# Clustered attention and two feed-forward layers: three weight pieces decoded in place, one multiply on another engine, and a new order around tiles 6 to 9

## Chip, cores and metric

One core of a Trainium2 chip runs the whole program. The metric is device microseconds of one execution, given as the median of several runs. Engines are named as in the profile: PE does matmuls (PEld is its loading of weights), DVE is the vector engine, ACT the scalar engine, POOL is GpSimd, and SP issues most of the DMAs, one after the other.

## What is computed

The reference has three stages, all in float32:

- Attention over 2 batches, 8 heads, 768 positions and 64 channels. Each query and key is assigned to the nearest of 16 centroids of its head (by cosine), and a query sees only keys of its own cluster. Scores are q k^T / 8, masked, then a softmax, then the product with v.
- A feed-forward layer on the 1536 x 512 result: h = x w_in (512 to 2048), a rational function P(h)/Q(h) of degree 3 over 2, then the product with w_out (2048 to 512).
- A mixture of eight experts (512 to 1024, relu, 1024 to 512). Their weights are a softmax over the experts, normalised eight times over rows and columns.

## The kernel before

Matmuls run in a reduced float32 form, so an operand is kept as a high part and a low part and one product takes three matmuls (lines 860 to 862). A weight tile is therefore "decoded" or "split" into two tiles, wh and wl.

**Attention** walks 8 pairs of heads (pair n is one batch and two heads). The loop counter is kk, 12 steps to a pair, 96 in all; in what follows "step x" is kk modulo 12. In each step kk PE makes scores of one tile of 128 queries against 768 keys (lines 391 and 392), DVE takes their maxima (397), ACT the exponential (405); four steps later PE transposes them (421), ACT and DVE split the transposed tile into high and low (430, 431), and three steps after that PE multiplies with v (444, 445). Operands of the next pairs are prepared by a list of pieces, one per step: transposes and splits of q and k (240, 250, 251), similarity to the centroids (264), and the choice of cluster in four steps: classify_m (284), classify_c (288, 289), classify_d (293) and classify_e (297), at steps 5 to 8. In classify_c the product `sv` is made on POOL, except for the first pair. The one-hot result goes through ACT (315, tile OHM) and four small DMAs (319) into the score operands sq2 and sk2 of the next pair; they are issued in step 10 and read by the first scores of the next pair.

SP is one queue in the order of the program. Per pair it issues: four loads of q and k for the pair after next (131, step 0); tb, which moves half of a result across partitions (514, steps 0, 3, 6 and 9); ten moves of operands st1, sq2, sk2 (336 to 340, in two groups, steps 2 and 3); rinv and rb, the reciprocals of the row sums (487, 491, step 3); v (138, step 4); the four OHM moves (319, step 10). POOL does, per pair, four additions x1f = ta + tb that wait for the tb move (515, issued two steps after it), twice the three operations of x_out (522 to 524, steps 8 and 9), and the split of v (350, 351; steps 4 and 10).

**Weights of the feed-forward layer** come as 32-bit words in pairs (`[..., 0]` and `[..., 1]`). decode has six operations: high and low on ACT (684, 687), shift on DVE (690), whole, upper and rest on POOL (693, 696, 699). Four half pieces, both halves of (0, 0) and of (0, 1) (unit, first or second weight), are decoded inside the attention loop by piece_w (729 to 752), with tiles of their own: raw, emag and etop, one buffer each. Their loads are issued at kk = 14, 28, 42 and 56; the six operations follow at 7 to 12 steps after. All other weights go through load_w, split_w and dp (661, 703): weight (1, 0) is loaded at kk = 88, weight (1, 1) at kk = 94; (1, 0) is decoded in five steps at kk = 100, in the list `end` (778) and at t = 1, 2, 3 of the next stage, and (1, 1) at t = 2 to 6.

**Feed-forward** has 48 tiles (512 tokens by 128 hidden units; tile n belongs to a unit of 256 hidden units). A step t issues, in the order of the program: act_b of tile t - 1 (901 to 906: square, abs, two affine forms on ACT, two products on POOL), act_steps of tile t - 2 and act_q of tile t - 1 on DVE, pieces of weights (key "w"), act_r of tile t - 1 (914, 915, ACT), then on PE stage1 of tile t (12 matmuls, tile h) and stage2 of tile t - 5 (12 matmuls into two tiles y). The results y of one step are emptied in the next one (list `late`). PSUM has three banks for y (h of tiles 0 to 2 use them first), three for h and two for q. A bank of h comes free with the last of act_steps (926).

At the seam, attention's PSUM pools (ps_s two tiles of two banks, ps_t two banks, ps_v and ps_p one each) are handed on to the three pools of the next stage. `rb_last` is a ps_s tile for the last reciprocals, `pt_31` another for transposes of the last group; rb_last is read by x_last (474).

Of the kernel before, what the change touches and what calls it, by code (L numbers as in the profile page):

```python
# [30 lines left out]
def kernel(  # L31
# [15 lines left out]
    nc = tc.nc  # L47
# [42 lines left out]
    def left(name, bufs):  # L90
        return ctx.enter_context(tc.tile_pool(name=name, bufs=bufs, reuse_waits="tile"))
# [84 lines left out]
        nc.vector.tensor_tensor(WG[:, :, E : 2 * E], wg, WG[:, :, 0:E].bitcast(F32), op=ALU.subtract)  # L176


    csq = one.tile([P, D], F32, name="csq")
    css = one.tile([P, 16], F32, name="css")[:, :1]  # L180
    nc.scalar.activation(csq, cen, AF.Square, accum_out=css)
    cnm = one.tile([P, 16], F32, name="cnm")[:, :1]
    gt(cnm, css, half[:, 0:1], op=ALU.pow)
    nc.vector.tensor_scalar(cnm, cnm, 1e-6, None, op0=ALU.add)
    crn = one.tile([P, 32], F32, name="crn")[:, :1]
    nc.vector.reciprocal(crn, cnm)
    cn2 = one.tile([P, 2, D], F32, name="cn2")
# [26 lines left out]
    def prep(n):  # L214
# [71 lines left out]
        def classify_c():  # L286
            sv = st["sv"] = one.tile([P, NB, C], F32, tag="sv", name=f"sv_{n}")
            nc.vector.tensor_tensor(sv, st["sims"], bc(st["mx"]), op=ALU.is_equal)
            (nc.vector.tensor_tensor if n == 0 else gt)(sv, sv, rev, op=ALU.mult)

        def classify_d():
            mk = st["mk"] = one.tile([P, 32], F32, tag="mk", name=f"mk_{n}")[:, :NB]
# [116 lines left out]

    def transposes(g, part):  # L410
        pss = []
        if g == NG - 1 and part == 0:
            last["pt"] = ps_s.tile([P, 2, 512], F32, tag="s", name=f"pt_{g}")
        for j in (2 * part, 2 * part + 1):
            if g == NG - 1 and part != 1:
                ps = last["pt"][:, j % 2]
            else:
                ps = ps_t.tile([P, 512], F32, tag="t", name=f"pt_{g}_{j}")
            for i in range(GT):
                pv_ = prob[g][i].rearrange("p a b -> p (a b)")  # L420
# [105 lines left out]
    def attention():  # L526
# [38 lines left out]
        for kk in range(END + LAGT + 9):  # L565
# [86 lines left out]
    def source(ui, i):  # L652
        m, e, u = units[ui]
        fs = slice(u * FU, (u + 1) * FU)
        if m == 0:
            src = moe_w_in[:, fs] if i == 0 else moe_w_out[fs, :]
            return src.bitcast(U32).rearrange("(c p) (f w) -> p c f w", p=P, w=2)
        src = moe2_w1[e][:, fs] if i == 0 else moe2_w2[e][fs, :]
        return src.rearrange("(c p) f -> p c f", p=P)

    def load_w(ui, i):
        if ui >= len(units):
            return
        if units[ui][0] == 0:
            t = stg.tile([P, *wshape[i], 2], U32, tag=f"stg{i}", name=f"stg_{ui}_{i}")
        else:
            t = sg2.tile([P, *wshape[i]], F32, tag=f"sg{i}", name=f"sg_{ui}_{i}")
        nc.sync.dma_start(t, source(ui, i))
        staged[ui, i] = t

    def weight_tiles(ui, i):
        shape = [P, *wshape[i]]
        return (
            wp[ui % 2].tile(shape, F32R, tag=f"wh{i}", name=f"wh_{ui}_{i}"),
            wp[ui % 2].tile(shape, F32R, tag=f"wl{i}", name=f"wl_{ui}_{i}"),
        )

    def decode(raw, mag, top, wh, wl):
# [47 lines left out]
    LASTK = 2 * NT * (NPR - 1)  # L726
    early = {}

    def piece_w(x, i, h):
        st = {}  # L730
        n = wshape[i][0] // 2
        c = slice(h * n, (h + 1) * n)
        shape = [P, n, wshape[i][1]]

        def load():
            st["raw"] = etp.tile([*shape, 2], U32, tag="raw", name=f"raw_{i}_{h}")
            nc.sync.dma_start(st["raw"], source(0, i)[:, c])

        def begin():
            if h == 0:  # L740
                weights[0, i] = weight_tiles(0, i)
            mag = etp.tile(shape, F32, tag="emag", name=f"emag_{i}_{h}")
            top = etp.tile(shape, F32, tag="etop", name=f"etop_{i}_{h}")
            st["fns"] = decode(st["raw"], mag, top, *(w[:, c] for w in weights[0, i]))

        early.setdefault(x, []).append(load)
        early.setdefault(x + 7, []).append(begin)
        for y, k in enumerate((7, 8, 9, 10, 11, 12)):
            early.setdefault(x + k, []).append(lambda y=y: st["fns"][y]())

    for y in range(4):
        piece_w(14 + 14 * y, y // 2, y % 2)

    mctx = ctx.enter_context(ExitStack())
    wp = [left("wp_0", 1)]
    etx = ctx.enter_context(ExitStack())
    etp = etx.enter_context(tc.tile_pool(name="etp", bufs=1, reuse_waits="tile"))
    for kk in attention():
        if isinstance(kk, list):
            end = kk  # L760
            break
        if kk == LASTK:
            pctx.close()
            etx.close()
            wp.append(left("wp_1", 1))
            stg = mctx.enter_context(tc.tile_pool(name="stg", bufs=1, reuse_waits="tile"))
            dp = mctx.enter_context(tc.tile_pool(name="dp", bufs=2, reuse_waits="tile"))
        if kk == LASTK + 4:
            load_w(1, 0)
        if kk == LASTK + 10:  # L770
            load_w(1, 1)
        for fn in early.pop(kk, ()):
            fn()
        if kk == GT * NG + 4:
            ahead = [(split_w(1, 0), 0), (split_w(1, 1), 1)]
            ahead[0][0].pop(0)()
    assert not early
    end.insert(1, ahead[0][0].pop(0))
    for fn in end:
        fn()  # L780
    sctx.close()
# [117 lines left out]
    def act_b(n):  # L899
        ps, q0, h2, uu, ww, _, _ = act[n]  # L900
        nc.scalar.activation(h2, ps, AF.Square)
        nc.scalar.activation(q0, ps, AF.Abs, scale=cf[:, 4:5])
        nc.scalar.activation(uu, ps, AF.Identity, scale=cf[:, 3:4], bias=cf[:, 2:3])
        nc.scalar.activation(ww, ps, AF.Identity, scale=cf[:, 1:2], bias=cf[:, 0:1])
        gt(uu, uu, h2, op=ALU.mult)  # L905
        gt(uu, uu, ww, op=ALU.add)
# [329 lines left out]
    for ui in range(NO):  # L1236
# [39 lines left out]
    for t in range(last):  # L1276
        if t == N1 + 2:
# [24 lines left out]
        for a in p.get("s1", ()):  # L1302
            stage1(*a)
        for fn in p.get("g", ()):
            fn()
        for ui, c, f in p.get("s2", ()):
            for i in range(4 * f // FT, 4 * (f + 1) // FT):
                stage2(ui, c, i)
# [45 lines left out]
```

## Time and profile before

| | |
|---|---|
| median of 3 runs | 1561.09 us (1558.44 to 1562.6) |
| the profiled execution | 1559.76 us |
| its span, first to last instruction | 1557.9 us |
| PE busy | 1529.0 us, 98% of the span |
| DVE, ACT, POOL busy | 1129.6, 650.2, 742.4 us |
| attention, from the span's start to the first matmul of tile 0 | 271.1 us |
| feed-forward, tiles 0 to 47 | to about 560 us |
| mixture of experts | the rest |

The profiled execution is 1.3 us under the median of the runs. The span leaves 1.9 us of the execution's time outside. PE's busy time counts matmuls from start to a modelled end, and those ends overlap with the next start, so a delay is read from the spacing of starts and from the idle time in brackets behind a row, not from the busy share. A bracket names what ended the idle time.

### The profile page before, as it was taken

What the parts mean: (1) busy time and instruction counts of PE and PEld (TensorE: products, weight loads), DVE (VectorE), ACT (ScalarE), POOL (GpSimd) and SP (SyncE); (2) the same over time, 40 slices, a digit from 0 to 9 for tenths busy, and PEclk for the clock granted to TensorE, in tenths of its full rate; (3) what the DMA queues carried; (4) which work ended last, traced back from release to release, by engine and by line L of the source; (5) the groups of instructions that cost most, each with busy time, mean ns of one, the idle gap of its engine ahead of it and who ended that gap; (6) DMA issues with size and microseconds to landing.
All of it is one profiled execution on the core that took longest, in us unless ns stands there. A gap on an engine that the chain in (4) does not pass through costs nothing.

```text
span 1557.9 us, 20894 instructions
## 1 busy us (share of the span) xinstructions
PE 1529.0 (98%) x7807; PEld 1351.4 (87%) x7807; DVE 1129.6 (73%) x1909; ACT 650.2 (42%) x1238; POOL 742.4 (48%) x633
## 2 busy tenths in 40 slices
PE   7999998899999999999999999999999999999998
PEld 5889898688888787888989999999999999998997
DVE  7888888678888748786666666667666666676666
ACT  5888887888887521221212121212121212121211
POOL 2254452888788763443444344434443444344420
PEclk9999999899999999999999999999999999999999
DMA  8567742211220010110011001101110101010102
GB/s 186 139 160 163 173 100 73 82 54 55 82 82 1 28 41 15 41 41 27 28 41 42 27 29 40 41 28 34 34 41 28 41 28 41 28 41 28 41 1 82
DMA packets 72574, 89.04 MB, mean 57 GB/s; under 512 B 30116, under 2 KB 50424, under 8 KB 72472
## 3 DMA queue, kind: packets, MB, share of 16 engines
q1 hardware_dynamic: 70904, 87.31, 20.3%
q8 instruction: 61, 1.00, 0.3%
q10 hardware_dynamic: 1568, 0.39, 0.1%
q14 instruction: 41, 0.34, 0.1%
HBM read 62.57 MB, written 3.19 MB: 42 GB/s over the span
## 4 chain that ended last, share of the span: by engine, by line
PE 91%; DVE 4%; POOL 2%; ACT 2%; issue 1%; DMA 1%; SPq 0%; ACTq 0%; POOLq 0%; DVEq 0%
PE y L860 14%; PE y L861 14%; PE y L862 14%; PE m L862 9%; PE m L860 9%; PE m L861 9%; PE pt L421 4%; PE h L861 4%; PE h L860 4%; PE h L862 4%; PE v L444 2%; PE v L445 2%; PE s L391 2%; PE s L392 2%; PE sim L264 1%
## 5 line engine op out<-in xcount | busy, mean ns | idle before, releaser
L972 DVE SCALAR_TENSOR_TENSOR acc<-y,gate,acc 128x512 f32<-128x512 f32 x348 | 260.8, 750 | 177.4 <-PE y L862 176.0
L860 PE MATMUL y<-wh,gh 128*128 128x512 f32 x696 | 270.9, 389 | 1.6 <-DVE acc L972 1.6
L862 PE MATMUL y<-wh,gl 128*128 128x512 f32 x696 | 271.9, 391 | 0.0
L861 PE MATMUL y<-wl,gh 128*128 128x512 f32 x696 | 271.8, 390 | 0.0
L1089 POOL TENSOR_TENSOR rl<-sg,rh 128x512 fp32r<-128x512 f32 x29 | 45.7, 1576 | 399.9 <-ACT rh L1081 399.9
L1166 ACT COPY c<-m 128x384 f32<-128x384 f32 x58 | 27.9, 482 | 455.9 <-PE m L862 455.9
L860 PEld LDWEIGHTS y<-wh,gh 128*128 128x128 f32 x696 | 130.7, 188 | 28.3 <-DVE acc L972 2.5
L862 PEld LDWEIGHTS y<-wh,gl 128*128 128x128 f32 x696 | 130.6, 188 | 27.3
L861 PEld LDWEIGHTS y<-wl,gh 128*128 128x128 f32 x696 | 130.6, 188 | 26.1
L1151 DVE SCALAR_TENSOR_TENSOR gl<-v,gh 128x384 fp32r<-128x384 f32 x174 | 119.4, 686 | 0.0
L1150 ACT ACTIVATE gh<-v 128x384 fp32r<-128x384 f32 x174 | 91.5, 526 | 60.9 <-DVE v L1189 29.2
L431 DVE TENSOR_TENSOR ptl<-pt,pth 128x384 fp32r<-128x384 f32 x192 | 97.6, 550 | 23.7 <-ACT pth L430 23.0
L860 PE MATMUL h<-XH,wh 128*128 128x512 f32 x264 | 104.3, 395 | 7.9 <-POOL uu L905 5.7
L714 POOL TENSOR_SCALAR wh<-sg 128x512 fp32r<-128x512 f32 x70 | 44.2, 631 | 136.9 <-PE y L862 131.4
L1150 ACT ACTIVATE gh<-u 128x384 fp32r<-128x384 f32 x58 | 30.6, 527 | 184.0 <-DVE u L1175 184.0
L861 PE MATMUL h<-XL,wh 128*128 128x512 f32 x264 | 104.3, 395 | 0.2 <-POOL XL L1300 0.2
L862 PE MATMUL h<-XH,wl 128*128 128x512 f32 x264 | 104.2, 395 | 0.0
L715 POOL TENSOR_TENSOR wl<-sg,wh 128x512 fp32r<-128x512 f32 x70 | 99.1, 1415 | 5.8
L430 ACT CAST pth<-pt 128x384 fp32r<-128x384 f32 x192 | 83.5, 489 | 38.2 <-PE pt L421 36.2
L397 DVE TENSOR_REDUCE nm<-s 128x1 f32<-128x768 f32 x96 | 91.3, 951 | 8.4 <-PE s L392 8.2
L405 ACT ACTIVATE pr<-s,nm 128x768 f32<-128x768 f32 x96 | 88.5, 922 | 3.2 <-DVE nm L397 3.1
L421 PE MATMUL pt<-ident,pr 128*128 128x128 f32 x576 | 83.2, 277 | 4.5 <-DVE ptl L431 4.4
(231 smaller groups left out, 4093.5 us busy)
## 6 DMA issues: line engine op xcount, KB each, us to landing
sg<-in_moe_w_dram SPq DMA_DIRECT2D x64, 512.0 KB, 3.4
stg<-in_moe_w_in_dram SPq DMA_DIRECT2D x7, 1024.0 KB, 5.4
stg<-in_moe_w_out_dram SPq DMA_DIRECT2D x7, 1024.0 KB, 5.4
st<-HQK SPq DMA_DIRECT2D x15, 384.0 KB, 4.5
qk<-in_q_dram SPq DMA_DIRECT2D x16, 192.0 KB, 3.6
vt<-in_v_dram SPq DMA_DIRECT2D x8, 384.0 KB, 5.0
out_dram<-acc SPq DMA_DIRECT2D x12, 256.0 KB, 2.0
st<-LQK SPq DMA_DIRECT2D x15, 192.0 KB, 4.6
```

The lines of the kernel that those rows point to most:

```text
L397: nc.vector.tensor_reduce(nm, ps[:, :, :HS], axis=AX.XY, op=ALU.max, negate=True)
L405: nc.scalar.activation(pr, ps[:, :, :HS], AF.Exp, bias=nm, accum_out=rss[n][:, x : x + 1])
L421: nc.tensor.transpose(ps[:, i * P : (i + 1) * P], pv_[:, j * P : (j + 1) * P], ident)
L430: nc.scalar.copy(th[:, jj, :], ps[:, :HS])
L431: nc.vector.tensor_tensor(tl[:, jj, :], ps[:, :HS], th[:, jj, :].bitcast(F32), op=ALU.subtract)
L715: gt(wl[:, c], raw[:, c], wh[:, c].bitcast(F32), op=ALU.subtract)
L860: nc.tensor.matmul(ps, ah, bh, start=first, stop=False)
L861: nc.tensor.matmul(ps, ah, bl, start=False, stop=False)
L862: nc.tensor.matmul(ps, al, bh, start=False, stop=last)
L972: nc.vector.scalar_tensor_tensor(a, ps, p, a, op0=ALU.mult, op1=ALU.add)
L1150: nc.scalar.activation(gh[:, f], c, AF.Relu)
L1151: soon.append(lambda: nc.vector.scalar_tensor_tensor(gl[:, f], c, 0.0, gh[:, f].bitcast(F32), op0=ALU.max, op1=ALU.subtract))
```

## The change

Six parts:

1. The three small tiles css, cnm and crn become columns of one tile, and the square of the centroids is written into cn2, which is overwritten later. This saves space.
2. sv is multiplied on DVE for every pair.
3. For group 30 the last two transposes go into a ps_s tile as well, and rb_last is taken two steps later, at kk = 98. As tiles alternate between the two buffers of ps_s, rb_last then lies in banks 0 and 1 (before: 2 and 3) and pt_31 in banks 2 and 3. The first h tile lies in bank 3 in both.
4. piece_w decodes in place: mag is raw[..., 1] and top is raw[..., 0], so emag and etop are gone, and the space goes to a pool for the first weight of odd units (wp_1a). It takes six half pieces, of (0, 0), (0, 1) and now (1, 0). Loads are issued at kk = 11, 23, 35, 47, 59 and 71, the six operations at 6, 7, 7, 8, 11 and 11 steps after, which is at steps 5, 6, 6, 7, 10 and 10 of the next pair. The tile raw has one buffer, as before. Weight (1, 0) is no longer decoded at the seam; (1, 1) is loaded at kk = 88 and decoded at t = 3 to 7.
5. act_b makes uu before q0.
6. In steps t = 5, 6 and 7 stage1 and stage2 are issued ahead of the activations and y is emptied at once; in t = 6, 7 and 8 stage2 comes before stage1. PE's order is then, with hN for stage1 of tile N and yN for stage2: h5 y0 y1 h6 y2 h7 y3 h8 h9 y4 (before: h5 y0 h6 y1 h7 y2 h8 y3 h9 y4).

```diff
@@ -176,15 +176,13 @@
-    css = one.tile([P, 16], F32, name="css")[:, :1]
...
+    crs = one.tile([P, 32], F32, name="crs")
+    css, cnm, crn = crs[:, 0:1], crs[:, 8:9], crs[:, 16:17]
+    cn2 = one.tile([P, 2, D], F32, name="cn2")
+    nc.scalar.activation(cn2[:, 0, :], cen, AF.Square, accum_out=css)
...
@@ -286,7 +284,7 @@
-            (nc.vector.tensor_tensor if n == 0 else gt)(sv, sv, rev, op=ALU.mult)
+            nc.vector.tensor_tensor(sv, sv, rev, op=ALU.mult)
@@ -409,10 +407,10 @@
-        if g == NG - 1 and part == 0:
+        if (g, part) in ((NG - 2, GT - 1), (NG - 1, 0)):
             last["pt"] = ps_s.tile([P, 2, 512], F32, tag="s", name=f"pt_{g}")
         for j in (2 * part, 2 * part + 1):
-            if g == NG - 1 and part != 1:
+            if g == NG - 2 and part == GT - 1 or g == NG - 1 and part != 1:
                 ps = last["pt"][:, j % 2]
@@ -584,7 +582,7 @@
-            elif kk == END:
+            elif kk == END + 2:
                 last["rb"] = ps_s.tile([P, 2, 512], F32, tag="s", name="rb_last")
@@ -670,9 +668,10 @@
+        pool = wp[ui % 2 * (1 + i)]
         return (
-            wp[ui % 2].tile(shape, F32R, tag=f"wh{i}", name=f"wh_{ui}_{i}"),
...
+            pool.tile(shape, F32R, tag=f"wh{i}", name=f"wh_{ui}_{i}"),
...
@@ -726,33 +725,34 @@
-            st["raw"] = etp.tile([*shape, 2], U32, tag="raw", name=f"raw_{i}_{h}")
-            nc.sync.dma_start(st["raw"], source(0, i)[:, c])
+            st["raw"] = etp.tile([P, n, wshape[i][1], 2], U32, tag="raw", name=f"raw_{ui}_{i}_{h}")
+            nc.sync.dma_start(st["raw"], source(ui, i)[:, c])
...
-            mag = etp.tile(shape, F32, tag="emag", name=f"emag_{i}_{h}")
-            top = etp.tile(shape, F32, tag="etop", name=f"etop_{i}_{h}")
-            st["fns"] = decode(st["raw"], mag, top, *(w[:, c] for w in weights[0, i]))
-
-        early.setdefault(x, []).append(load)
-        early.setdefault(x + 7, []).append(begin)
-        for y, k in enumerate((7, 8, 9, 10, 11, 12)):
+            raw = st["raw"]
+            st["fns"] = decode(
+                raw, raw[..., 1].bitcast(F32), raw[..., 0].bitcast(F32), *(w[:, c] for w in weights[ui, i])
+            )
+
+        early.setdefault(x - 1, []).append(load)
+        early.setdefault(x + 5, []).append(begin)
+        for y, k in enumerate((5, 6, 6, 7, 10, 10)):
             early.setdefault(x + k, []).append(lambda y=y: st["fns"][y]())
 
-    for y in range(4):
-        piece_w(14 + 14 * y, y // 2, y % 2)
+    for y, (ui, i) in enumerate(((0, 0), (0, 1), (1, 0))):
+        for h in range(2):
+            piece_w(2 * NT * (2 * y + h + 1), ui, i, h)
...
-    wp = [left("wp_0", 1)]
+    wp = [left("wp_0", 1), left("wp_1a", 1)]
@@ -762,20 +762,15 @@
-            wp.append(left("wp_1", 1))
+            wp.append(left("wp_1b", 1))
...
         if kk == LASTK + 4:
-            load_w(1, 0)
-        if kk == LASTK + 10:
             load_w(1, 1)
...
-        if kk == GT * NG + 4:
-            ahead = [(split_w(1, 0), 0), (split_w(1, 1), 1)]
-            ahead[0][0].pop(0)()
     assert not early
-    end.insert(1, ahead[0][0].pop(0))
+    ahead = split_w(1, 1)
@@ -899,8 +894,8 @@
         nc.scalar.activation(h2, ps, AF.Square)
+        nc.scalar.activation(uu, ps, AF.Identity, scale=cf[:, 3:4], bias=cf[:, 2:3])
         nc.scalar.activation(q0, ps, AF.Abs, scale=cf[:, 4:5])
-        nc.scalar.activation(uu, ps, AF.Identity, scale=cf[:, 3:4], bias=cf[:, 2:3])
@@ -1252,9 +1247,8 @@
-    for fns, x in ahead:
-        for y, fn in enumerate(fns):
-            at(x + y + 1, "w", fn)
+    for x, fn in enumerate(ahead):
+        at(x + 3, "w", fn)
@@ -1280,6 +1274,25 @@
+        def firsts_():
+            for a in p.get("s1", ()):
+                stage1(*a)
+            for fn in p.get("g", ()):
+                fn()
+
+        def seconds_():
+            for ui, c, f in p.get("s2", ()):
+                for i in range(4 * f // FT, 4 * (f + 1) // FT):
+                    stage2(ui, c, i)
+
+        soon = LAG1 <= t < LAG1 + 3
+        if soon:
+            for fn in (firsts_, seconds_) if t == LAG1 else (seconds_, firsts_):
+                fn()
+            for fn in late:
+                fn()
+            late.clear()
...
@@ -1299,13 +1312,12 @@
...
+        if t == LAG1 + 3:
+            seconds_()
+            firsts_()
+        elif not soon:
+            firsts_()
+            seconds_()
```

## Rows read from the trace of the kernel before

**Rows 1.** The page, part 1: busy time of PE and PEld.

```profile
PE 1529.0 (98%) x7807; PEld 1351.4 (87%) x7807; DVE 1129.6 (73%) x1909; ACT 650.2 (42%) x1238; POOL 742.4 (48%) x633
```

**Rows 2.** Windows: length, then busy PE, PEld, DVE, ACT, POOL, PEclk, DMA share, GB/s.

```profile
125.60:134.40 8.80, 8.63 (x60) 7.78 (x59) 8.70 (x16) 7.58 (x19) 2.02 (x2) 1.00 0.95 220
290.00:330.00 40.00, 34.34 (x142) 27.86 (x142) 28.96 (x43) 38.49 (x64) 34.68 (x24) 0.91 0.23 79
330.00:560.00 230.00, 229.33 (x1009) 188.89 (x1008) 182.99 (x288) 171.46 (x261) 191.54 (x136) 1.00 0.15 49
```

**Rows 3.** Waits: engine line <- awaited line: us, times, longest us.

```profile
DVE mk L293 <- POOL sv L289: 2.8, 3, 1.6
```

**Rows 4.** Waits of SP, its own queue, same columns.

```profile
SPq L668 <- DVE mag L690: 201.6, 12, 23.2
```

**Rows 5.** Timeline of SP, pair 5 of attention: start us, us, instruction.

```profile
170.11 1.31 SPq L131 DMA_DIRECT2D qk<-in_q_dram  x2
...
172.91 0.72 SPq L514 DMA_DIRECT2D tb<-ta  x1
176.44 0.52 SPq L224 DMA_DIRECT2D st<-HQK  x1
...
192.44 4.42 SPq L514 DMA_DIRECT2D tb<-ta  x2
...
198.91 0.56 SPq L224 DMA_DIRECT2D sq<-OHM  x1
```

**Rows 6.** Timeline of PE, first scores of pairs 5 and 6.

```profile
170.70 0.42 PE L391 MATMUL s<-st 128*128 128x384 f32 x1
...
201.98 0.42 PE L391 MATMUL s<-st 128*128 128x384 f32 x1
```

**Rows 7.** Timeline of POOL, late in pair 3 and in pair 5.

```profile
135.42 1.00 POOL L515 TENSOR_TENSOR x1f<-ta,tb 64x384 f32<-64x384 f32 x1 [5.79 <-DMA tb<-ta]
...
143.40 1.01 POOL L515 TENSOR_TENSOR x1f<-ta,tb 64x384 f32<-64x384 f32 x1
...
196.72 1.02 POOL L515 TENSOR_TENSOR x1f<-ta,tb 64x384 f32<-64x384 f32 x1 [3.02 <-DMA tb<-ta]
```

**Rows 8.** Groups by line and form up to 262 us: count | busy, mean ns.

```profile
L699 POOL TENSOR_TENSOR wl<-emag,wh 128x512 fp32r<-128x512 f32 x4 | 5.2, 1291 | 0.0
...
L696 POOL TENSOR_SCALAR wh<-emag 128x512 fp32r<-128x512 f32 x4 | 2.5, 620 | 0.3
...
L690 DVE TENSOR_SCALAR emag<-raw 128x512 uint32<-128x512 uint32 x4 | 2.4, 592 | 0.0
...
L289 DVE TENSOR_TENSOR sv<-sv,rev 128x384 f32<-128x384 f32 x1 | 0.6, 560 | 0.0
```

**Rows 9.** Timeline, the seam of attention and feed-forward, PE and ACT.

```profile
259.69 1.01 PE L421 MATMUL pt<-ident,pr 128*128 128x128 f32 x6 [0.89 <-DVE ptl L431]
...
268.48 0.44 PE L445 MATMUL v<-ptl,vs 128*128 128x384 f32 x1
...
271.11 0.52 PE L860 MATMUL h<-XH,wh 128*128 128x512 f32 x1 [2.19 <-DVE x1f L474]
...
271.43 0.63 PE L861 MATMUL h<-XL,wh 128*128 128x512 f32 x1
...
271.86 0.63 PE L862 MATMUL h<-XH,wl 128*128 128x512 f32 x1
...
275.72 0.60 ACT L901 ACTIVATE h<-h 128x512 f32<-128x512 f32 x1 [4.21 <-PE h L862]
```

**Rows 10.** Timeline, tiles 5 to 8 of feed-forward, PE and ACT.

```profile
291.66 0.39 PE L861 MATMUL y<-hl,wh 128*128 128x512 f32 x1
291.89 0.39 PE L862 MATMUL y<-hh,wl 128*128 128x512 f32 x1
297.94 0.77 PE L860 MATMUL h<-XH,wh 128*128 128x512 f32 x1 [5.66 <-POOL uu L905]
...
313.87 0.60 ACT L901 ACTIVATE h<-h 128x512 f32<-128x512 f32 x1 [0.65 <-PE h L862]
```

More of the change, by code (lines that the diff above doesn't have):

```diff
@@ L176, in constants @@
         nc.vector.tensor_tensor(WG[:, :, E : 2 * E], wg, WG[:, :, 0:E].bitcast(F32), op=ALU.subtract)
-    csq = one.tile([P, D], F32, name="csq")
-    css = one.tile([P, 16], F32, name="css")[:, :1]
-    nc.scalar.activation(csq, cen, AF.Square, accum_out=css)
-    cnm = one.tile([P, 16], F32, name="cnm")[:, :1]
+    crs = one.tile([P, 32], F32, name="crs")
+    css, cnm, crn = crs[:, 0:1], crs[:, 8:9], crs[:, 16:17]
+    cn2 = one.tile([P, 2, D], F32, name="cn2")
+    nc.scalar.activation(cn2[:, 0, :], cen, AF.Square, accum_out=css)
     gt(cnm, css, half[:, 0:1], op=ALU.pow)
     nc.vector.tensor_scalar(cnm, cnm, 1e-6, None, op0=ALU.add)
-    crn = one.tile([P, 32], F32, name="crn")[:, :1]
     nc.vector.reciprocal(crn, cnm)
-    cn2 = one.tile([P, 2, D], F32, name="cn2")
     for j in range(2):
@@ L672, in weight_tiles @@
         shape = [P, *wshape[i]]
+        pool = wp[ui % 2 * (1 + i)]
         return (
-            wp[ui % 2].tile(shape, F32R, tag=f"wh{i}", name=f"wh_{ui}_{i}"),
-            wp[ui % 2].tile(shape, F32R, tag=f"wl{i}", name=f"wl_{ui}_{i}"),
+            pool.tile(shape, F32R, tag=f"wh{i}", name=f"wh_{ui}_{i}"),
+            pool.tile(shape, F32R, tag=f"wl{i}", name=f"wl_{ui}_{i}"),
         )
@@ L727, with piece_w @@
     early = {}
-    def piece_w(x, i, h):
-        st = {}
+    def piece_w(x, ui, i, h):
         n = wshape[i][0] // 2
         c = slice(h * n, (h + 1) * n)
-        shape = [P, n, wshape[i][1]]
+        st = {}
         def load():
-            st["raw"] = etp.tile([*shape, 2], U32, tag="raw", name=f"raw_{i}_{h}")
-            nc.sync.dma_start(st["raw"], source(0, i)[:, c])
+            st["raw"] = etp.tile([P, n, wshape[i][1], 2], U32, tag="raw", name=f"raw_{ui}_{i}_{h}")
+            nc.sync.dma_start(st["raw"], source(ui, i)[:, c])
         def begin():
             if h == 0:
-                weights[0, i] = weight_tiles(0, i)
-            mag = etp.tile(shape, F32, tag="emag", name=f"emag_{i}_{h}")
-            top = etp.tile(shape, F32, tag="etop", name=f"etop_{i}_{h}")
-            st["fns"] = decode(st["raw"], mag, top, *(w[:, c] for w in weights[0, i]))
-        early.setdefault(x, []).append(load)
-        early.setdefault(x + 7, []).append(begin)
-        for y, k in enumerate((7, 8, 9, 10, 11, 12)):
+                weights[ui, i] = weight_tiles(ui, i)
+            raw = st["raw"]
[5 more added lines that the diff above has]
+        for y, k in enumerate((5, 6, 6, 7, 10, 10)):
             early.setdefault(x + k, []).append(lambda y=y: st["fns"][y]())
-    for y in range(4):
-        piece_w(14 + 14 * y, y // 2, y % 2)
+    for y, (ui, i) in enumerate(((0, 0), (0, 1), (1, 0))):
+        for h in range(2):
+            piece_w(2 * NT * (2 * y + h + 1), ui, i, h)
     mctx = ctx.enter_context(ExitStack())
-    wp = [left("wp_0", 1)]
+    wp = [left("wp_0", 1), left("wp_1a", 1)]
     etx = ctx.enter_context(ExitStack())
@@ L1301 @@
         xs.clear()
[L1302 to L1308, printed above, removed]
+        if t == LAG1 + 3:
[4 more added lines that the diff above has]
+            seconds_()
         for ui, i in p.get("W", ()):
```

## Prediction, made before the changed kernel was seen to run

> **What bounds the kernel now.** I read the page first: PE is busy for 98% of the span [rows 1], so only stretches in which PE loses time can give anything, and anything that makes PE wait costs in full. Then the windows by stage: from 330 to 560 us PE is busy 229.33 of 230 us [rows 2], and the experts behind are as full. What can be won lies before 330 us: at the seam and in the first tiles of feed-forward, where PE is busy 34.34 of 40 us while ACT is busy 38.49 [rows 2], and in attention. There PE is rarely idle, but its three helpers are nearly as full: in steps 6 to 9 of a pair DVE is busy 8.70 of 8.80 us [rows 2]. Then the waits, to see who holds whom, the timelines of SP and POOL in attention, and PE's timeline at the seam.
>
> **The sum, part by part**, made against the profiled execution (1559.76 us; its span is 1557.9 us). The median of the runs shown is 1561.09, or 1.3 us more; I add that at the end.
>
> **sv on DVE.** The wait that goes: classify_d on DVE waited for sv on POOL three times, 2.8 us in total, the longest 1.6 [rows 3]. Behind each stands a DVE without slack, so PE pays that and an after-effect; I take 2.8 to 4.5 us gained. What comes: 0.56 us of DVE [rows 8] for six pairs in just the steps in which DVE is full, and with it now the shift of a half piece, 0.59 us [rows 8], at step 6 as well (before, its four shifts fell on other steps). DVE's 0.1 us of slack and PE's double-buffered transposes hide about half of these 1.15 us; the other 0.6 to 0.7, times six, is 3.6 to 4.2 us lost, bounded by 0 and 6.9. Sum for DVE in attention: 0, between -4.5 and +4.
>
> **The load of a half piece: a new wait on SP.** This is the step that decides. The tile raw has one buffer. Before, shift was the last to read it, 5 steps ahead of the next load. Now rest on POOL reads it, issued at step 10, and the next load is issued at step 11. SP stops at a DMA whose buffer isn't free: it stood 201.6 us over 12 loads in the next stage for such a release [rows 4]. So I follow rest. On POOL the addition of step 8 starts at 196.72 [rows 7], 26.0 us after its pair's first scores at 170.70 [rows 6]. Behind it in the queue are x_out twice and the split of v; in pair 3 these last from 135.42 to 143.40, 8.0 us [rows 7]. Then upper, 0.62, and rest, 1.29 [rows 8], with 0.1 between: rest ends 10.0 us after that addition starts, and 36.0 us after the pair's start. A pair lasts 31.3 us [rows 6], of which I take 31.1 without the waits for sv. So SP waits until 4.9 us into the next pair, while it was free to go on before that pair began.
>
> Behind the load on SP stand four loads of q and k and tb, which take from 170.11 to 173.63, 3.5 us [rows 5], and the load itself, 0.7 (one issue as long as one of q). So the first st move comes 9.1 us into the pair and not 176.44 - 170.70 = 5.7 [rows 5, 6]: 3.4 us late. From there SP has no pause until tb of step 6, 16.0 us later at 192.44 [rows 5], and for this tb waits the addition of step 8, 4.3 us after its issue [rows 5, 7]. That closes a ring: load 0.7, q, k and tb 3.5, moves 16.0, landing 4.3, POOL 10.0 = 34.5 us, against a pair of 31.1. Each of the five loads that can wait (kk = 23, 35, 47, 59, 71) so puts SP back by another 3.4 us.
>
> PE feels it through the OHM moves, needed by the next pair's first scores. SP issues them at 198.91; with tb of steps 6 and 9 (0.9 and 0.5) it would have been ready at 193.8 [rows 5], so 5.1 us are slack. The five rounds cost 0, then 6.8 - 5.1 = 1.7, 3.4, 3.4, and 0.7 in pair 6, which has no more q and k to load (2.7 less). Sum 9.2; I take 8.5, for 0.5 us or so between landing and use. Bounds: a ring 1 us shorter makes it 5, one longer 13.
>
> By the rows the in-place operands cost nothing more: shift already reads every second word, 592 ns for 512 columns, which is less by column than the packed sv, 560 for 384 [rows 8]. POOL on every second word isn't in the trace; I take its packed prices, as lower bound too, and as upper bound 0.3 us for each of the two, the 13 us end above. [...]
>
> ACT's six lots of high and low fall on steps 5 and 6 in place of four on others; I count them with DVE's.
>
> **Transposes in ps_s.** PE waited 0.89 us for a ps_t bank [rows 9]; that goes, but the two halves of one ps_s tile are then emptied with less overlap. I take 0.5 us gained, of 0 to 1.
>
> **rb_last in another bank.** The first h matmul began 2.19 us late, at 271.11, when x_last had read rb_last [rows 9]. It needs bank 3, which pt_31 now holds, and pt_31 is empty before the last v matmul at 268.48 [rows 9] can start. What is late next is that matmul itself: 2.2 us gained.
>
> **The clock at the seam.** [...] ACT could begin at 275.72, 4.6 us after PE [rows 9]; at the full clock twelve starts and the last one's end make 11 x 0.23 + 0.39 = 2.9, and 3.0 with the signal. With PE not idle I expect the full clock: 1.6 us gained.
>
> **Tiles 0 to 8.** From 275.72 ACT goes on without a wait for PE until 313.87 [rows 9, 10], and PE's stop of 5.66 us at 297.94 [rows 10] is a wait for the end of this chain (square, q0, uu, Ln, Exp, then four operations on DVE, then h's bank). The decode of (1, 0) taken out there was POOL's and, before 271, ACT's; ACT has as much to do as before. So the new order cannot give more than ACT's earlier start, already counted: PE's one long stop becomes several of 1 to 2 us (before y1, for the bank of h2; before h6 and h7), and the end of the stretch stays 38 us after ACT's first square. uu before q0 helps POOL by 0.66 us a tile and puts DVE's q off by as much: 0. I count 0 here, between -2.5 and +2 (the clock may fall again).
>
> Part 1 is 0: nothing waits for its columns.
>
> Sum: 0 + 8.5 - 0.5 - 2.2 - 1.6 + 0 = +4.2, or 1564.0 for the profiled execution, and 1565 beside the median. 0.3% of the time is 4.7 us, about what a measurement of this kernel can tell from no change.
>
> **The rivals.**
> *A: the ring doesn't bind.* If rest ends sooner than I read (in steps 6 to 9 POOL is busy 2.02 of 8.80 us [rows 2]), or SP's stretch of 16 us shrinks when its sources are long ready, then the load waits for a while and SP catches up before the OHM moves. For it speaks a slack of 5.1 us [rows 5], against it that POOL's chain is all of durations and one landing. The time: -4.3 us, 1555.5, or 1557 beside the median; with the better end of sv and of the tiles, 1552. This is the side of faster.
> *B: the ring is longer.* Place: upper and rest on POOL in every round; price: 0.6 us or more each round, or as much on SP when its DMAs crowd; it decides as soon as a ring exceeds 35 us. Four rounds add 2.5 to 4.5 and more: 1568 to 1573.
> *C: new stops at the seam trip the clock.* Each fall at tiles 5 to 8 could cost 1.8 us (nine starts at 0.43 in place of 0.23); it adds to any of these and decides none.
>
> **How the numbers follow.** Forecast 0.6, A 0.25, B 0.15; C has no share of its own. The forecast alone spans 1560 to 1570. The range over all is 1554 to 1573, which leaves out A's better end and B's worse. Faster by over 0.3% is under 1556.4: nearly half of A and a little of the forecast, where the ring is short and the tiles better, 0.2. Slower is over 1565.8: a bit under half of the forecast and all of B, 0.4. Within: 0.4.
>
> **What would show it.** In the trace after: SP's load of raw waits for POOL's wl (rest) at kk = 23 to 71, by some 5 us in the first round; the tb of step 6 comes later in its pair from pair to pair; PE stands before a pair's first `s<-sk,sq` or ACT before ta, by 2 to 4 us, in pairs 3 to 6; the first scores of pair 7 come some 8 us later than before. DVE has no wait for sv. h begins within 0.3 us of the last v matmul, at full clock. If pair 7 begins no later than before, rival A is right; if PE's stops between tiles 5 and 9 sum to under 3 us, my reading of ACT's chain is wrong.

## The result, and the profile after

The change makes the kernel slower. Its median is 1575.31 us of 5 runs (1572.3 to 1576.63), beside 1560.08 us of 5 runs before; the ratio is 1.0093, with a 95% interval of 1.0078 to 1.0109. The forecast was 1565 within 1554 to 1573, so the time lies above the range. The profiled execution took 1574.15 us (span 1572.3), 14.4 more than the 1559.76 before.

In the changed kernel the lines from 391 to 474 are two lower (scores are L389 and L390), raw is loaded on L735, and wl of a half piece (rest) is made on L698. The page, parts 1 and 4; the first line answers to [rows 1]:

```profile
PE 1532.3 (97%) x7807; PEld 1350.5 (86%) x7807; DVE 1132.1 (72%) x1917; ACT 651.7 (41%) x1240; POOL 734.6 (47%) x629
...
PE 85%; DVE 4%; ACT 4%; DMA 3%; POOL 2%; issue 1%; SPq 0%; ACTq 0%; POOLq 0%; DVEq 0%
```

No engine is busy for more than 3.3 us longer than before, and none has a larger share. In the chain that ended last, though, PE has 85% (before: 91%), and ACT and DMA hold 7% between them (before: 2 and 1%). So the time has gone into waits. The waits of SP's queue first (engine line <- awaited line: us, times, longest us):

```profile
SPq L735 <- POOL wl L698: 45.7, 5, 10.7
SPq L489 <- DMA rinv<-rt: 17.6, 7, 3.4
```

And those of the other engines:

```profile
POOL x1f L513 <- DMA tb<-ta: 139.5, 20, 23.5
...
ACT ta L511 <- POOL x1f L513: 17.8, 11, 2.6
PEld v L442 <- ACT ta L511: 10.9, 6, 2.4
```

Read downwards, from the first of these rows, this is the new mechanism: SP stands at the load of raw until rest is done, five times and 45.7 us; the moves tb behind it land late, and POOL's additions wait for them 139.5 us (before: 80.1); ACT may not write the next ta (it has two buffers) until an addition has read an old one; and PE's product with v waits for ACT. The last two rows have no counterpart in the trace of the kernel before, nor in that of e1_load_late below; POOL's wait by itself says little, for there it is 99.4 us and nothing is lost. The wait `DVE mk <- POOL sv` of [rows 3] is gone.

One round of it in SP's timeline, which answers to [rows 5] (start us, us, instruction); pair 4 runs from 145.02 to 181.16:

```profile
155.35 0.34 SPq L735 DMA_DIRECT2D raw<-in_moe_w_out_dram  x1
155.73 1.30 SPq L131 DMA_DIRECT2D qk<-in_q_dram  x2
...
159.25 0.91 SPq L512 DMA_DIRECT2D tb<-ta  x1
160.26 0.54 SPq L222 DMA_DIRECT2D st<-HQK  x1
...
176.85 1.54 SPq L512 DMA_DIRECT2D tb<-ta  x2
178.48 0.56 SPq L222 DMA_DIRECT2D sq<-OHM  x1
...
191.76 0.38 SPq L735 DMA_DIRECT2D raw<-in_moe_w_in_dram  x1
```

Here is the other half of the round, POOL's timeline; its first row answers to [rows 7], its last to [rows 8]:

```profile
181.68 1.00 POOL L513 TENSOR_TENSOR x1f<-ta,tb 64x384 f32<-64x384 f32 x1 [5.54 <-DMA tb<-ta]
...
190.42 1.31 POOL L698 TENSOR_TENSOR wl<-raw,wh 128x512 fp32r<-128x512 f32 x1
```

Rest ends at 191.73, and 0.03 us later SP issues the next load. From load to load it is 191.76 - 155.35 = 36.4 us; the others took 35.6, 36.0 and 36.2. And PE, with the two places at which it pays in this pair:

```profile
145.02 0.42 PE L389 MATMUL s<-st 128*128 128x384 f32 x1
...
166.22 0.44 PE L442 MATMUL v<-pth,vs 128*128 128x384 f32 x1 [2.03 <-ACT ta L511]
...
175.59 0.44 PE L442 MATMUL v<-pth,vs 128*128 128x384 f32 x1 [1.61 <-ACT ta L511]
...
181.16 0.42 PE L389 MATMUL s<-st 128*128 128x384 f32 x1
182.95 0.41 PE L390 MATMUL s<-sk,sq 80*128 80x384 f32 x1 [1.36 <-DMA sq<-OHM]
```

The pair lasts 181.16 - 145.02 = 36.1 us, where pair 5 of [rows 6] lasted 31.3. So the starts of the pairs tell the whole story. In us, taken from the first scores of each pair in PE's timeline: the columns 1 to 6 are the lengths of these pairs (pair 0, left out, lasts 27.3 us before and 27.9 in the other two). The third line belongs to the first experiment below:

| | pair 0 starts | 1 | 2 | 3 | 4 | 5 | 6 | pair 7 starts | from 0 to 7 |
|---|---|---|---|---|---|---|---|---|---|
| before | 17.32 | 32.64 | 31.44 | 30.89 | 31.09 | 31.29 | 29.56 | 231.54 | 214.2 |
| after | 19.84 | 31.52 | 31.73 | 34.00 | 36.14 | 37.03 | 30.41 | 248.60 | 228.8 |
| e1_load_late | 18.50 | 31.29 | 31.67 | 31.27 | 31.29 | 31.84 | 31.01 | 234.79 | 216.3 |

The seam, which answers to [rows 9], in the timelines of PE and of ACT:

```profile
287.35 0.44 PE L443 MATMUL v<-ptl,vs 128*128 128x384 f32 x1 [0.15 <-DVE ptl L429]
287.63 0.39 PE L855 MATMUL h<-XH,wh 128*128 128x512 f32 x1
287.86 0.40 PE L856 MATMUL h<-XL,wh 128*128 128x512 f32 x1
...
290.56 0.60 ACT L896 ACTIVATE h<-h 128x512 f32<-128x512 f32 x1 [0.53 <-PE h L857]
```

The first h matmul now starts 0.28 us after the last one with v, the next 0.23 us later (before: 2.63 and then 0.32 and 0.43), and ACT's first square comes 2.9 us after h in place of 4.6. The granted clock is 1.00 from 287.6 to 290.6 us; before, from 271.43 to 274.42 with the starts 0.43 us apart, it was 0.50.

### The profile page after: what moved, and what is told of

It is laid out like the page before. It is cut to its first block, busy times and chain, and to the rows that moved or that the text cites. A ratio compares the mean times of both kernels' runs of the same rounds, so it can differ in the third digit from the quotient of the medians.

```text
span 1572.3 us, 20912 instructions
## 1 busy us (share of the span) xinstructions
PE 1532.3 (97%) x7807; PEld 1350.5 (86%) x7807; DVE 1132.1 (72%) x1917; ACT 651.7 (41%) x1240; POOL 734.6 (47%) x629
## 3 DMA queue, kind: packets, MB, share of 16 engines
q10 hardware_dynamic: 1568, 0.39, 0.1%
HBM read 62.57 MB, written 3.19 MB: 42 GB/s over the span
## 4 chain that ended last, share of the span: by engine, by line
PE 85%; DVE 4%; ACT 4%; DMA 3%; POOL 2%; issue 1%; SPq 0%; ACTq 0%; POOLq 0%; DVEq 0%
PE y L856 13%; PE y L857 13%; PE y L855 13%; PE m L857 9%; PE m L855 9%; PE m L856 9%; PE h L856 3%; PE h L857 3%; PE h L855 3%; PE pt L419 3%; PE v L442 1%; PE v L443 1%; PE s L389 1%; PE s L390 1%; DMA tb<-ta 1%
## 5 line engine op out<-in xcount | busy, mean ns | idle before, releaser
L1161 ACT COPY c<-m 128x384 f32<-128x384 f32 x58 | 27.9, 482 | 454.8 <-PE m L857 454.8
L855 PEld LDWEIGHTS y<-wh,gh 128*128 128x128 f32 x696 | 130.7, 188 | 27.3 <-DVE acc L967 1.4
L857 PEld LDWEIGHTS y<-wh,gl 128*128 128x128 f32 x696 | 130.6, 188 | 27.3
L429 DVE TENSOR_TENSOR ptl<-pt,pth 128x384 fp32r<-128x384 f32 x192 | 97.8, 550 | 35.6 <-ACT pth L428 34.7
L513 POOL TENSOR_TENSOR x1f<-ta,tb 64x384 f32<-64x384 f32 x28 | 28.5, 1016 | 147.1 <-DMA tb<-ta 139.5
```

Of the source, the lines that this page charges most:

```text
L429: nc.vector.tensor_tensor(tl[:, jj, :], ps[:, :HS], th[:, jj, :].bitcast(F32), op=ALU.subtract)
L855: nc.tensor.matmul(ps, ah, bh, start=first, stop=False)
L857: nc.tensor.matmul(ps, al, bh, start=False, stop=last)
```

## The experiments

The theory was the ring: the load of a half piece stands on SP until rest has read raw, and everything that SP issues behind it is late. The first rival was the work itself: sv and the shifts on a full DVE, high and low on ACT, all in the same steps. All ratios are to the kernel before, run on the same chip.

**The ring opened on SP's side.** The load is issued three steps later, when rest is done.

```diff
-        early.setdefault(x - 1, []).append(load)
+        early.setdefault(x + 2, []).append(load)
```

> The kernel after, with the load of a half piece issued three steps later (step 2 of the pair in place of step 11 of the pair before), when rest is done. Ring theory (SP stands at the load until rest has read raw, and everything behind it on SP is late): SP's wait for wl falls from 45.7 us to under 8 us, pairs 3 to 6 last 30.9 to 31.6 us again, pair 7 starts 213 to 216 us after pair 0 (after: 228.8; before: 214.2), the time falls by 12 to 15 us to 1559 to 1562. Rival theory (sv and the shifts on a full DVE, high and low on ACT in the same two steps, lengthen the pairs): pairs 3 to 6 stay at 33 us or more and the time over 1570.

It took 1558.75 us, ratio 0.9991 (0.9981 to 1.0). The one line gives back all that the change had lost. Pairs 3 to 6 last 31.0 to 31.8 us and pair 7 starts 216.3 us after pair 0 (table above), each a little over what was expected. Raw is now loaded 10.3 us into every pair, as late as in the worst rounds of the kernel after (10.6), and ACT, its first reader, waits for it 0.2 us in all: raw that comes late costs next to nothing here. And among SP's waits there is none for wl; the first of those in attention are

```profile
SPq L512 <- ACT pth L428: 28.3, 21, 3.5
SPq L222 <- ACT HQK L248: 22.8, 8, 4.9
SPq L489 <- DMA rinv<-rt: 19.4, 7, 3.6
```

waits for ACT's ordinary work and for a landing. Between the two kernels nothing differs in what the engines compute, so the rival falls.

**The ring opened on POOL's side.** The load stays where it is, and upper and rest come two steps earlier.

```diff
-        for y, k in enumerate((5, 6, 6, 7, 10, 10)):
+        for y, k in enumerate((5, 6, 6, 7, 8, 8)):
```

> The kernel after, with upper and rest issued at step 8 in place of step 10, ahead of the second x_out and the split of v on POOL; the load stays at step 11. Ring theory: POOL's part of the ring shrinks by the 4 to 6 us of what rest no longer stands behind, from 36 to 30 to 32 us, so it no longer binds or by under 1 us a round: SP's wait for wl under 12 us in all, pair 7 starts 214 to 218 us after pair 0, time 1560 to 1565. Rival theory (work on DVE and ACT in steps 5 and 6 lengthens the pairs): no change, 1572 to 1576.

1559.98 us, ratio 1.0004 (0.9995 to 1.0014). SP's wait has shrunk to

```profile
SPq L735 <- POOL wl L698: 2.7, 4, 1.3
```

and from pair 0 to pair 7 it is 234.82 - 17.75 = 217.1 us. Two edits that have nothing in common but the ring both end the loss.

**The load on another queue.** The step stays, and POOL issues the load instead of SP.

```diff
-            nc.sync.dma_start(st["raw"], source(ui, i)[:, c])
+            nc.gpsimd.dma_start(st["raw"], source(ui, i)[:, c])
```

> The kernel after with the load of raw issued from POOL's queue instead of SP's, at the same step 11: it still comes after rest, which POOL itself did before, and nothing on SP stands behind it. Ring theory (the cost is what is blocked on SP, not the late raw itself): the pairs go back to 31 to 32 us, pair 7 starts 214 to 219 us after pair 0, 1559 to 1564 us, with some us open for POOL's time to issue. Rival (the load that comes late delays high, low and shift, and these the rest): pairs 3 to 5 stay at 34 us or more, over 1570.

1566.05 us, ratio 1.0044 (1.003 to 1.0058): outside what either theory had said. Pairs 3 to 5 last 31.3, 32.3 and 31.7 us although raw is still loaded only after rest, so it is SP's standing that costs, and little of it the late raw. (That little: in pairs 4 to 6 raw lands 7.6 to 8.0 us after its issue, ACT waits for it 2.8 us in three places, and step 6 lasts 2.91, 2.19 and 2.14 us in place of 1.90.) But pair 1 lasts 36.1 us, 4.8 more than in e1_load_late. Its first scores, in the timelines of POOL and of PE:

```profile
44.76 0.93 POOL L735 DMA_DIRECT2D raw<-in_moe_w_in_dram  x1
...
51.46 0.41 PE L390 MATMUL s<-sk,sq 80*128 80x384 f32 x1 [3.05 <-DMA sk<-OHM]
```

POOL had nothing to wait for in the first round and issued the 512 KB at 44.76, together with the four OHM moves (44.74 to 47.20). Two of these, whose landing the trace shows, landed 6.0 and 5.2 us after their issue; in the kernel after, where the same load stands behind them on SP, 2.1. PE stood for it, and its scores behind it (54.49, 54.81, 55.13) start 0.32 us apart and not 0.18, as at 57.56, 57.74 and 57.92. In later rounds, where the load starts behind them, they landed in 2.1 to 2.8 us again. So SP's order had also kept the large load off the small moves here; but POOL's load also goes through another kind of queue (software_dynamic in the page, where SP's is hardware_dynamic), and whether that has a part in it is not shown.

**sv back on POOL, with the ring.**

```diff
-            nc.vector.tensor_tensor(sv, sv, rev, op=ALU.mult)
+            (nc.vector.tensor_tensor if n == 0 else gt)(sv, sv, rev, op=ALU.mult)
```

> The kernel after, with sv back on POOL. Ring theory: the load on SP still waits for rest; sv on POOL comes ahead of the addition that the ring waits for, so the ring is as long or up to 0.7 us longer: 1573 to 1579. Rival theory (0.66 us more of DVE in full steps is what lengthens the pairs): 3 to 5 us faster, 1569 to 1571.

1573.88 us, ratio 1.0091 (1.0076 to 1.0106), inside what the ring had said. One thing neither theory had said, in the waits of SP and of DVE:

```profile
SPq L735 <- POOL wl L698: 21.7, 5, 5.0
...
DVE mk L291 <- POOL sv L287: 13.8, 4, 4.5
```

SP's wait has halved and the time has not moved: pairs 2 to 5 still last 34.6 to 37.3 us. sv stands behind an addition on POOL that waits for a late tb, DVE waits for sv, and PE's stop has moved to step 8. What a ring costs is its length less the length of a pair; the size of any one wait in it says little.

**sv without the ring.** The same edit on top of e1_load_late:

> The load three steps later (as in e1_load_late) with sv back on POOL: part 2 of the change alone, without the ring. The prediction's sum for DVE (0, from -4.5 to +4): step 7 falls from 3.19 us to about 2.6 (0.6 us for six pairs, 3.6 us gained), and DVE waits for sv on POOL again at step 8 (0.3 to 0.6 us in most pairs, 2 to 4 us lost): 1556 to 1560. Theory that the waits for sv cost much more than 0.66 us of DVE: 1561 or more. Theory that they cost nothing: 1555 or less.

1560.83 us, ratio 1.0006 (0.9997 to 1.0015): 2 us slower than e1_load_late and above what the sum had expected, so in the changed kernel sv is better on DVE, by a little. DVE waits for sv 8.3 us in six places. And the other way round, part 2 alone on the kernel before (the diff is part 2's own line):

> The kernel before with part 2 alone: sv on DVE for every pair. The prediction's sum for it was 0 (from -4.5 to +4), with the waits for sv (2.8 us in three) gone and 0.6 to 0.7 us more in each of six pairs. In e9_mid, with sv on DVE and no shift in step 7, pairs 1 to 4 last 31.2 us, as in the kernel before (31.1 to 31.3): ratio 0.999 to 1.001. Theory that sv on DVE is a gain by itself (e1_load_late against e6_late_sv_pool: 2.1 us): 0.9985 or less. Theory that it is a loss hidden by the rest: 1.0015 or more.

1561.28 us, ratio 1.0009 (0.9999 to 1.0018): nothing, or at most 2.8 us lost.

**The pieces where the engines have slack.**

```diff
-        early.setdefault(x - 1, []).append(load)
-        early.setdefault(x + 5, []).append(begin)
-        for y, k in enumerate((5, 6, 6, 7, 10, 10)):
+        early.setdefault(x - 5, []).append(load)
+        early.setdefault(x + 3, []).append(begin)
+        for y, k in enumerate((3, 3, 4, 4, 5, 5)):
```

> The kernel after with each half piece's load at step 7 of the pair before, high and low at step 3, shift and whole at step 4, upper and rest at step 5, where DVE, ACT and POOL have slack (in e1_load_late DVE is busy 1.4 of 2.65 us in step 4 and POOL is idle in steps 4 to 6). Rest is done two steps ahead of the next load, so no ring; and step 7 loses the shift: 2.4 to 2.7 us in place of 3.19, for six pairs 3 to 4.6 us less than e1_load_late: 1554 to 1556. Rival (sv alone fills DVE in step 7, and where the shift stands is the same to PE): 1558 to 1560.

1557.95 us, ratio 0.998 (0.9971 to 0.9989), between the two. Step 7 lasts 3.10 to 3.15 us in pairs 1 to 4, hardly less than 3.19, but 2.86 and 2.85 in pairs 5 and 6. DVE and POOL at step 7 of pair 4 and of pair 5 show why:

```profile
158.51 1.01 POOL L513 TENSOR_TENSOR x1f<-ta,tb 64x384 f32<-64x384 f32 x1 [3.91 <-DMA tb<-ta]
...
159.09 0.85 DVE L287 TENSOR_TENSOR sv<-sv,rev 128x384 f32<-128x384 f32 x1
...
190.32 0.56 DVE L287 TENSOR_TENSOR sv<-sv,rev 128x384 f32<-128x384 f32 x1
...
190.87 1.00 POOL L513 TENSOR_TENSOR x1f<-ta,tb 64x384 f32<-64x384 f32 x1 [5.03 <-DMA tb<-ta]
```

Where POOL's addition is under way, sv takes 0.85 us; where it comes after, 0.56. The shift is gone from the step, and the earlier pieces have brought the addition into sv. This was in neither theory.

**Part 3 undone** (on e1_load_late, the diff is part 3 backwards):

> The load three steps later (as in e1_load_late) with part 3 undone: the last transposes of group 30 in ps_t, rb_last taken at kk = 98. The prediction priced part 3 at 0.5 + 2.2 and the half clock behind it at 1.6, 4.3 us in all: 1562 to 1563.5 if all of it is shown, h 2 us or more behind the last v matmul and its starts 0.43 us apart. Rival (ACT is free only later, so PE's late start at the seam is hidden): 1558 to 1560.

1563.66 us, ratio 1.0021 (1.0013 to 1.003), 4.9 us above e1_load_late by the medians and 4.7 by the ratios. The seam is as it was before, in PE's timeline:

```profile
271.96 0.44 PE L443 MATMUL v<-ptl,vs 128*128 128x384 f32 x1
274.24 0.76 PE L855 MATMUL h<-XH,wh 128*128 128x512 f32 x1 [1.84 <-DVE x1f L472]
...
275.23 0.63 PE L857 MATMUL h<-XH,wl 128*128 128x512 f32 x1
275.66 0.63 PE L855 MATMUL h<-XH,wh 128*128 128x512 f32 x1
```

h comes 2.28 us after v, and its matmuls 0.43 us apart. Nothing downstream hides it: from ACT's first square to the end of the span it is 1281.7 us in both. The two traces, each of one execution, differ by less than the medians, 1.8 us up to the first h and 1.4 from there to ACT's first square.

**The old order of tiles 5 to 9**, with q0 ahead of uu, first on the kernel after, then on e1_load_late:

```diff
-        soon = LAG1 <= t < LAG1 + 3
+        soon = False
...
-        if t == LAG1 + 3:
+        if False:
```

> The kernel after, with the old order of tiles 5 to 9 and q0 ahead of uu, all else as after. Theory of the prediction (ACT's chain sets the end of these tiles, and the order only cuts PE's one long stop into several): one stop of PE of 4 us or more before the first y in place of two of about 2, the end of the stretch within 2.5 us either way: 1572 to 1577. Rival theory (the order shortens the stretch): 1578 or more.

> The load three steps later (as in e1_load_late) and, in addition, the old order of tiles 5 to 9 with q0 ahead of uu. By the reading that ACT's chain sets the end of these tiles: within 2.5 us of e1_load_late's 1558.75 either way, and by e4_old_order's trace (10.6 us lost between starts of matmuls from 280 to 360 us where after lost 11.4) rather 1 to 2 us faster: 1556.5 to 1559. Theory that the new order shortens the stretch: 1561 or more.

1572.95 us with the ring (ratio 1.0087, 1.007 to 1.0104) and 1557.46 without (0.9979, 0.997 to 0.9988): 0.9 and 1.9 us less than with the new order, by the ratios (0.0006 and 0.0012 of 1560). Neither is clear of the noise by itself (the intervals reach 0.0017 and 0.0009 to either side). But e10_mid_old_order below has the same sign against e9_mid (0.0008), and from ACT's first square to the end of the span the four traces of the changed kernel with the old order take 1279.6 to 1280.9 us, the eight with the new one 1281.7 to 1282.7. The new order's stops of PE in the kernel after are

```profile
308.55 0.50 PE L855 MATMUL y<-hh,wh 128*128 128x512 f32 x1 [1.70 <-ACT acc L951]
313.59 0.50 PE L855 MATMUL h<-XH,wh 128*128 128x512 f32 x1 [1.99 <-DVE hl L921]
320.09 0.50 PE L855 MATMUL h<-XH,wh 128*128 128x512 f32 x1 [0.76 <-DVE hl L921]
329.25 0.50 PE L855 MATMUL h<-XH,wh 128*128 128x512 f32 x1 [0.67 <-DVE hl L921]
335.42 0.50 PE L855 MATMUL h<-XH,wh 128*128 128x512 f32 x1 [0.44 <-DVE hl L921]
341.78 0.50 PE L855 MATMUL h<-XH,wh 128*128 128x512 f32 x1 [0.63 <-DVE hl L921]
```

6.2 us in six, and in e4_old_order there is one (before an h, where it had been expected before the first y):

```profile
311.89 0.79 PE L855 MATMUL h<-XH,wh 128*128 128x512 f32 x1 [4.79 <-DVE hl L921]
```

Behind that one stop matmuls start 0.42 to 0.43 us apart (312.49, 312.91, 313.34, 313.76); in the kernel before, such starts behind the stop of 5.66 us [rows 10] went with a granted clock of 0.50, from 298.5 to 301.9 us. In the kernel after the granted clock is 1.00 from 286 to 345. So the new order keeps PE at the full clock and still gains nothing.

**Together.** e9_mid with the old order, and this with sv on POOL:

> The best of what ran so far together: e9_mid with the old order of tiles 5 to 9 and q0 ahead of uu. If the two add (the order gave 1.3 us in e5_late_old_order against e1_load_late), 1556 to 1557.5; if the new order gives as much as it takes, 1557.5 to 1559.

> e10_mid_old_order with sv back on POOL. In e6_late_sv_pool the wait for sv had grown to 8.3 us, with whole on POOL in the same steps; here POOL has no piece of weight after step 5. If that was the reason, the wait for sv is back at some 3 us (before: 2.8), step 7 at 2.6 us or less, and the time 1554 to 1557. If sv waits behind the additions anyway, steps 7 and 8 together last as long or longer than on DVE and it is 1557 to 1560.

e10_mid_old_order took 1554.5 us, ratio 0.9972 (0.996 to 0.9983): below both expectations and the lowest of all versions, though its interval overlaps those of e9_mid and e5_late_old_order. By the ratios it is 4.4 us below the kernel before and some 19 below the kernel after (0.9972 / 1.0093 = 0.988). It keeps parts 1 to 4 of the change, with other steps for the pieces. With sv on POOL it is 1562.11 us (1.0014, 1.0006 to 1.0023), above both expectations; upper and rest now stand ahead of sv in POOL's queue, and DVE waits:

```profile
163.51 0.66 POOL L695 TENSOR_SCALAR wh<-raw 128x512 fp32r<-128x512 f32 x1
164.25 1.30 POOL L698 TENSOR_TENSOR wl<-raw,wh 128x512 fp32r<-128x512 f32 x1
165.52 1.01 POOL L287 TENSOR_TENSOR sv<-sv,rev 128x384 f32<-128x384 f32 x1
166.56 0.55 DVE L291 TENSOR_REDUCE mk<-sv 128x24 f32<-128x384 f32 x1 [1.68 <-POOL sv L287]
```

My reason for e11 was wrong: POOL had pieces of weights in those steps after all, since they had slipped behind the additions.

## Why the prediction was wrong, and where it was right

The sum was +4.2 us and the profiled execution shows +14.4. By its steps, in us:

| step | predicted | measured | from |
|---|---|---|---|
| load of a half piece (ring) | +8.5 (5 to 13) | +14.1 | pairs 0 to 7, after less e1_load_late: 12.5, and 1.6 in pair 7 |
| sv and the rest of DVE in attention | 0 (-4.5 to +4) | +2.1 | e1_load_late less before, 216.3 - 214.2; of it 1.5 in e1_load_late alone, see DVE below |
| ps_s transposes, rb_last | -2.7 | -2.2 | pair 7's start to first h, 39.0 - 1.6 of the ring, beside 39.6 |
| clock at the seam | -1.6 | -1.7 | first h to ACT's first square, 2.93 and 4.61 |
| tiles 0 to 8, and all behind | 0 (-2.5 to +2) | -0.4 | ACT's first square to the span's end |
| start of pair 0 | none | +2.5 | 19.84 and 17.32; no part of the change, see below |

**The step that failed** is the price of the ring: "load 0.7, q, k and tb 3.5, moves 16.0, landing 4.3, POOL 10.0 = 34.5 us, against a pair of 31.1". The mechanism, its place and its first round were right: SP waited 5.0 us in the first round (forecast: some 5), then 8.6, 10.6, 10.7 and 10.7. The length was not. The same terms in the round shown above: load, q, k and tb 160.26 - 155.35 = 4.9 for 4.2; moves 176.85 - 160.26 = 16.6 for 16.0; landing 181.68 - 176.85 = 4.8 for 4.3; POOL 191.73 - 181.68 = 10.05 for 10.0; and the signal back, 0.03. So POOL, for which I had kept the upper bound, was exact, and the 1.9 us that were missing lie on SP and in the DMAs, which I had taken from a pair in which they ran undisturbed. The prediction says that SP has no pause in the 16.0 us, and that is not so: it sends rinv on, as rb, only after rinv has landed. In pair 5 before, that took 3.7 us from issue to issue (181.03 to 184.76), in the ring's round 4.4 (165.05 to 169.43), which is the whole growth of that term. A ring of 36 against a pair of 31.3 loses 4.7 a round and not 3.4. The rounds, as pair after less the same pair of e1_load_late: 0.1, 2.7, 4.9, 5.2, and 1.0 in pairs 6 and 7 together (-0.6, from step 2 of e1_load_late, and 1.6), where I had 0, 1.7, 3.4, 3.4 and 0.7. The shape holds, each round is half as much again. My upper bound let only POOL's two operations grow; it should have let SP and the landing grow as well.

**Where PE pays** was half right. I let it pay through the OHM moves, with 5.1 us of slack; these cost PE 1.36 us in the row above and 2.4 in all. Most came through ta, for which PE stood 8.9 us in six places: in pair 3, 2.4 of the 2.7 us lost stand in step 10. I named ACT before ta as a sign but gave it no slack of its own, and it gave way first.

**The rivals.** B, the longer ring, is what happened, at 1568 to 1573 with a chance of 0.15; it had the right mechanism and a price that still was too small. A, no ring, fell. Of C nothing shows: h kept the full clock (starts 0.23 us apart, granted clock 1.00 up to 345 us).

**DVE.** The sum of 0 came out as +2.1, inside its bounds; of part 2 by itself e13_before_sv_dve says +1.4 (from 0 to 2.8). By steps, e1_load_late less before: step 7 lasts 3.19 us in place of 2.42 in six pairs, 4.6 lost (forecast 3.6 to 4.2); step 8 gives back 2.1, steps 0 and 10 another 1.5 (forecast 2.8 to 4.5, all of it for sv); and step 2 adds 1.3. It lasts 3.97, 4.15 and 4.19 us in pairs 2, 5 and 6, where rest on POOL runs beside a small operation of DVE's (last section), and 3.58 or 3.59 in the kernel after. So some 1.5 us of the 2.1 come with the late load and not with the change, and the ring cost as much more than 14.1. The row that I took for sv, 0.56 us, holds only where POOL lets it (0.75 to 0.92 us in three of the eight of the kernel after), and the shift's 0.59 was a mean of one at 1.17 beside POOL and three at 0.36 to 0.42. The in-place operands, words 8 bytes apart, cost next to nothing, as taken: upper 0.66 us for 0.62, rest 1.31 for 1.29.

**The seam and the tiles** came out as argued, to 0.6 us. e8_late_old_banks gives 4.7 to 4.9 us for part 3 with the clock by its runs, and 3.2 in the traces, where I had 4.3. The 1.6 us for the clock stood on starts 0.43 us apart [rows 9] against 0.23 [rows 10], and the traces show the granted clock at 0.50 in the first of these places and at 1.00 in the second, and 1.00 for h in the kernel after. The stops between tiles 5 and 9 sum to 6.2 us, over the 3 that would have refuted the reading of ACT's chain, and undoing the order changes the time by 1 to 2 us, inside the bounds and to the order's disadvantage, though no single comparison is clear of the noise.

## What to carry to other kernels

When an operation becomes the last reader of a tile with one buffer, follow the next DMA into that tile: here SP stood 45.7 us at five such loads, what stood behind them on its queue was delayed with them, and as part of that fed the same operation, there was a ring of 36.4 us whose excess over the period of 31.3 was paid every round. Place such a load in the queue behind the step at which the buffer is really free; here three steps were worth 16 us by the runs (0.0102 of 1560). When you sum up a ring from rows of an undisturbed pair, take the sum as its lower end (34.5 us here, where 36.4 were measured), and let the DMA terms, not only the engines', grow in the bound (moves 16.6 us for 16.0, landing 4.8 for 4.3, POOL 10.05 for 10.0).

## What was not expected of the hardware

- **DVE and POOL hold each other up.** sv on DVE takes 0.56 us alone (all six from 60 to 240 us in e1_load_late); in the kernel after it takes 0.75, 0.81 and 0.92 when an operation of POOL's of 1.0 us (an addition twice, the split of v in the last) began 0.66, 0.63 and 0.51 us ahead; in e10_mid_old_order step 7 lasts 2.85 us with sv at 0.56, 3.07 at 0.77, 3.27 at 0.97 and 3.48 at 1.19. In the kernel after it was once the other way: sv started 0.02 us ahead, kept its 0.56, and the addition took 1.38 us. The rows:

```profile
164.25 0.56 DVE L287 TENSOR_TENSOR sv<-sv,rev 128x384 f32<-128x384 f32 x1
...
164.27 1.38 POOL L513 TENSOR_TENSOR x1f<-ta,tb 64x384 f32<-64x384 f32 x1 [7.99 <-DMA tb<-ta]
...
164.72 1.22 DVE L689 TENSOR_SCALAR raw<-raw 128x512 uint32<-128x512 uint32 x1
```

  The shift behind it took 1.22 us, and 0.42 in most other pairs. The same befell a small operation on the row sums in e1_load_late, where rest began 0.07 us ahead of it; step 2 of that pair lasts 0.6 us longer:

```profile
145.51 0.16 DVE L450 TENSOR_SCALAR rs<-rs 128x12 f32<-128x12 f32 x1
...
208.57 1.31 POOL L698 TENSOR_TENSOR wl<-raw,wh 128x512 fp32r<-128x512 f32 x1
...
208.64 1.27 DVE L450 TENSOR_SCALAR rs<-rs 128x12 f32<-128x12 f32 x1
```

  sv has two inputs; the shift and the operation on the row sums, with one tile as input each, took longer as well (1.22 us for 0.42, 1.27 for 0.16). I had taken sv's price from the one row in which POOL was little in its way.
- **The start scatters by 3 us.** The first scores come at 17.3 to 20.3 us in the profiled executions of these kernels (18.7 in e13_before_sv_dve, which has the prologue of the kernel before; 17.3 in e3_sv_pool, which has that of the kernel after). So 2.5 us of the 14.4 between the two profiles belong to no part of the change; the 18 runs of the kernel before beside e10_mid_old_order lie from 1557.15 to 1562.08 us, 0.3% apart, so a smaller difference needs medians of several runs.
- **Small moves beside a large load** landed 5.2 and 6.0 us after issue in e12_gpsimd_queue, with 512 KB issued at the same time on POOL's queue, in place of 2.1 in the kernel after (above).
